# A fused attention and token-mixing kernel: where the dense matmuls of the late odd attention units stand between the logits, weighing and second logits

## The chip, the core and the metric

The kernel runs on one core of a Trainium2 chip. The metric is the device time of one execution in microseconds (us), with all inputs and the output in the chip's main memory. A core has TensorE (matmuls, PE in the profile; its weight loads are PEld), VectorE (DVE), ScalarE (ACT), GpSimd (POOL) and SyncE (SP), which here issues nearly all of the DMAs. Each works through its own list of instructions in order, and they wait for each other by semaphores. TensorE writes into PSUM, which has 8 banks here numbered 0 to 7.

## The reference

One sequence of 2048 tokens with 1024 features. It is normalised (xn), and the output is the sum of the input, an attention branch and a token-mixing branch.

```python
xn = _layernorm(x)                            # x: [1, 2048, 1024] bf16
return x + A(xn, wq, wk, wv, wo, beta) + B(xn, w1, b1, w2, b2)

# A: 32 heads of 32, 4 segments of 512 tokens, one after the other
for s in range(4):
    qs, ks, vs = q[:, :, s], k[:, :, s], v[:, :, s]
    p = softmax(qs @ ks.T * scale + causal_mask)
    a_dot = p @ vs
    a_mem = (phi(qs) @ M) / (phi(qs) @ z + 1e-6)     # memory of the earlier segments
    outs.append(g * a_mem + (1 - g) * a_dot)         # g = sigmoid(beta), one for each head
    M += phi(ks).T @ vs;  z += phi(ks).sum(tokens)
A = concat(outs) @ wo

# B: an MLP over the token dimension
B = (gelu(layernorm(xn).T @ w1 + b1) @ w2 + b2).T    # 2048 -> 3584 -> 2048
```

`phi(t)` is `t + 1` where t > 0, else `exp(t)`.

## The kernel before

First comes branch B (some 390 us). The attention follows, in `attention` (L1531), as a loop over 32 units. Unit u is one segment (u // 8) and one group of four heads (u % 8). Each unit issues, in program order, four kinds of work for TensorE:

- **Logits** (`logits(u, step)`, L1349). Keys times queries of four heads, transposed (keys on partitions), each head on 32 rows of the array, in blocks of 128 keys. Step 0 is key block 0 against 512 queries; step 1 is blocks 1 and 3 (384 and 128 queries); step 2 is block 2 of unit u and of unit u+1 together (256 queries each), so that only even units have a step 2. Each step writes PSUM banks 0 to 3, then one ScalarE instruction (L1370) exponentiates all four banks into pT. GpSimd then zeroes the part above the diagonal of each block (`affine_select`, L1374, the mask). Every logits step waits until the exp of the step before has read the banks. pT has two copies, for even and for odd units.
- **Weighing** of the unit before (`weigh(u - 1, part)`, L1379): many narrow matmuls of pT with the values (and one with the memory for each 128 queries). Part 0 writes bank 4, part 1 bank 5, part 2 bank 4 again, which must have been drained by VectorE (L1424, tile `ost`). Part 1 is the first that needs key block 2 of unit u-1. In the first three segments part 2 also updates the memory (L1435, L1437).
- **Dense jobs**: eight accumulating matmuls 128x512 each, in banks 6 and 7 by turns (`dense(n)`, L1326, issues the next n matmuls of the job queue). They are projections for later units (`q_job`, `k_job`, `v_job`) and output products of finished segments (`wo_job`). At its end each job has its bank read: by ScalarE for qT and vA (L1253, L1299), by VectorE for fin (L1313). The next job but one needs that bank.
- **Side steps**, a queue of VectorE and SyncE work: `combine(u - 1)` (L1440: scales, products, sum), the DMA transpose of its result into oT, the feature map phi of the queries, and others. `dense` takes one of them from the queue when a job reaches one of its stops (L1503, L1504).

How many dense matmuls go where is laid down by `cut(total, shares)` (L1604), which divides the unit's dense matmuls in proportion to a tuple. For an odd unit the places are: ahead of step 0, between step 0 and weighing part 0, between parts 0 and 1, between parts 1 and 2, between part 2 and step 1, and behind step 1. An even unit has one place more, between steps 1 and 2. From unit 18 on a quota (L1502) sets the total: with the jobs at hand an odd unit has 20 dense matmuls, 16 in unit 31. With 20, the third tuple below gives an odd unit 4, 2, 2, 2, 1, 9; with 16, it gives 4, 1, 1, 2, 0, 8. Unit 18 starts at about 531 us, unit 31 at about 627 us. After the loop, `tail` (L1612) weighs the last unit and finishes the last segment's output products; the transposed result of unit 30 is read there by the products that take row block 6 of wo.

```python
            if u >= 18 and even:
                cuts = self.cut(total, (0, 5, 1, 4, 0, 9, 5))
            elif u < 10 or u >= 14 and total <= 26:
                cuts = self.cut(total, (0, 4, 2, 4, 1, 13, 8) if even else (7, 3, 2, 4, 1, 15))
            else:
                cuts = self.cut(total, (0, 4, 2, 2, 2, 14, 8) if even else (7, 3, 2, 2, 2, 16))
```

Of the kernel before, what the change touches and what calls it, by code (L numbers as in the profile page):

```python
# [386 lines left out]
class _Kernel:  # L387
# [1143 lines left out]
    def attention(self):  # L1531
        self.jobs, self.turn, self.left = deque(), 0, 0
        self.side, self.stops = deque(), self.STOPS
        self.exps, self.in_etmp = [], [None] * 4
        self.wo_jobs = deque((c, half) for c in range(4 * (N_SEG - 1)) for half in range(2))
        self.jobs.extend([self.q_job(0), self.k_job(0)] + [self.v_job(0, c) for c in range(4)])
        self.dense(16)
        self.late_exps()
        self.phi_k(0)
        self.k_transpose(0)  # L1540
        self.jobs.extend([self.q_job(1), self.k_job(1)])
        self.dense(100)
        for u in range(N_UNIT):
            if u == N_GRP:
                t, R = _Walk(self.mem, self.B_AT + self.STG_AT, self.B_AT + self.S2_AT).take(
                    "oT2", [P, N_GRP, SEG_L], BF16, N_GRP)
                self.oT.append(t)
                self.R_oT.append(R)
                self.load_fin(0)
                self.load_fin(1)  # L1550
            if 1 <= u <= N_GRP:
                self.fw.dma(self.wo[:, u - 1, :], self.A_wo[(u - 1) * P:u * P, :], writes=[self.R_wo[u - 1]])
            even = u % 2 == 0
            self.jobs.extend(self.unit_jobs(u))
            total = 8 * len(self.jobs) - sum(j[0] for j in self.jobs) - self.left
            xn = self.XN_AT.index(u) + 4 if u in self.XN_AT else None
            if u in self.XN_AT[::4]:
                self.xn_load(xn)
                self.xn_load(xn + 1)
            if u >= 18 and even:  # L1560
                cuts = self.cut(total, (0, 5, 1, 4, 0, 9, 5))
            elif u < 10 or u >= 14 and total <= 26:
                cuts = self.cut(total, (0, 4, 2, 4, 1, 13, 8) if even else (7, 3, 2, 4, 1, 15))
            else:
                cuts = self.cut(total, (0, 4, 2, 2, 2, 14, 8) if even else (7, 3, 2, 2, 2, 16))
            end = u >= N_UNIT - 4
            self.stops = self.STOPS_FEW if total <= 26 and u >= 14 else self.STOPS
            self.dense(cuts[0])
            self.logits(u, 0)
            self.dense(cuts[1], end)  # L1570
            while end and self.side:
                self.side.popleft()()
            if u:
                self.weigh(u - 1, 0)
            self.dense(cuts[2], False)
            if u:
                self.weigh(u - 1, 1)
            self.dense(cuts[3], False)
            if u:
                self.weigh(u - 1, 2)  # L1580
                steps = self.combine(u - 1)
                last = steps[-1]
                steps[-1] = lambda u=u, last=last: (last(), self.o_transpose_dma(u - 1))
                self.side.append(steps.pop(0))
            if N_GRP <= u:
                self.side.append(lambda u=u: self.phi_q(u))
            if u:
                self.side.extend(steps)
            if u + 1 < N_UNIT:
                self.side.append(lambda u=u: (self.phi_k(u + 1), self.k_transpose(u + 1)))  # L1590
            if xn is not None:
                self.side.append(lambda c=xn: (self.xn_scale(c), self.xn_transpose(c), c % 4 < 2 and self.xn_load(c + 2)))
            self.dense(cuts[4])
            self.logits(u, 1)
            if even:
                self.dense(cuts[5])
                self.logits(u, 2)
            self.dense(8 * len(self.jobs) - sum(j[0] for j in self.jobs) - self.left)
        while self.side:
            self.side.popleft()()  # L1600
        self.tail()
# [84 lines left out]
```

## Time and profile before

| | us |
|---|---|
| median of 4 executions (651.43 to 651.85) | 651.59 |
| the profiled execution | 651.64 |
| its span, first to last instruction | 649.9 |
| TensorE busy | 645.4 |
| VectorE busy | 434.7 |
| ScalarE busy | 282.4 |
| GpSimd busy | 152.3 |

The span is some 1.7 us shorter than the time, which includes what lies around the program. The page divides the span into 40 slices of about 16 us, a digit for the busy tenths of each:

```profile
PE   9999999999999999999999999999999999999998
DVE  6885676665556664744637326766887888787896
ACT  6643222232210000110101037778777878889770
POOL 2410000000001220220202203343334444454440
PEclk9999999999999999999999999999999999999999
```

The last 15 or so slices are the attention: VectorE and ScalarE are busy for seven to nine tenths there, less in the stage ahead of it. The groups of instructions with the largest parts in the attention outside TensorE are these (columns: busy us, mean ns of one, then the idle time of the engine ahead of it and what ended most of it):

```profile
L1370 ACT ACTIVATE pT<-ps_all 128x2048 bf16<-128x2048 f32 x80 | 150.2, 1877 | 43.3 <-PE ps_all L199 42.7
L1374 POOL TENSOR_SCALAR_AFFINE_SELECT pT<-pT 128x512 bf16<-128x512 bf16 x128 | 103.8, 829 | 161.6 <-ACT pT L1370 161.6
L1424 DVE TENSOR_TENSOR ost<-ps_all,eps 128x396 bf16<-128x396 f32 (+1 forms) x72 | 36.9, 521 | 26.2 <-PE ps_all L199 25.7
L1473 DVE TENSOR_TENSOR prod<-ost,srec 128x1024 bf16<-128x1024 bf16 (+1 forms) x31 | 35.9, 1159 | 0.3
```

In a timeline the first two columns are the start and the length in us; an `x` with a number is how many instructions of one kind stand in the piece, and a bracket gives the engine's idle time ahead of it and what ended it.

### The profile page before, as it was taken

How to read it: one execution, taken by the hardware profiler on the slowest of the kernel's cores; microseconds unless marked ns; L12 is line 12 of the kernel's file. 1: busy time of each engine (PE TensorE's matmuls, PEld its weight loads, DVE VectorE, ACT ScalarE, POOL GpSimd, SP SyncE). 2: the span in 40 equal slices, each digit the busy share in tenths (PEclk: the TensorE clock that was granted, in tenths of full speed). 3: DMA queues.
4: the chain of work that ended last, by engine and by line, in shares of the span. 5: the costliest groups of instructions: out<-in, count | busy, mean ns of one | idle time of the engine just before them, and what ended most of it. 6: DMA issues, size and time to landing. Idle time of an engine off the chain costs nothing.

```text
span 649.9 us, 11189 instructions
## 1 busy us (share of the span) xinstructions
PE 645.4 (99%) x4611; PEld 303.9 (47%) x4611; DVE 434.7 (67%) x813; ACT 282.4 (43%) x307; POOL 152.3 (23%) x179
## 2 busy tenths in 40 slices
PE   9999999999999999999999999999999999999998
PEld 3444444444444444444444444444455454445544
DVE  6885676665556664744637326766887888787896
ACT  6643222232210000110101037778777878889770
POOL 2410000000001220220202203343334444454440
PEclk9999999999999999999999999999999999999999
DMA  8804233233488947538272957989863675445334
GB/s 302 217 0 131 66 103 92 65 111 85 126 259 196 239 119 210 147 112 227 73 219 84 267 124 179 191 166 215 145 142 94 161 164 123 125 103 129 101 97 139
DMA packets 190123, 95.00 MB, mean 146 GB/s; under 512 B 108664, under 2 KB 176248, under 8 KB 190072
## 3 DMA queue, kind: packets, MB, share of 16 engines
q1 hardware_dynamic: 189928, 94.25, 57.7%
q8 instruction: 36, 0.59, 0.4%
q14 instruction: 15, 0.12, 0.1%
q10 hardware_dynamic: 144, 0.03, 0.0%
HBM read 69.23 MB, written 11.53 MB: 124 GB/s over the span
## 4 chain that ended last, share of the span: by engine, by line
PE 94%; DMA 2%; ACT 2%; DVE 1%; SPq 0%; issue 0%
PE ps_all L199 94%; ACT pT L1370 1%; DMA w2s<-in_B_w_dram 1%; DMA w1early<-in_B_w_dram 1%; DVE sum L648 0%; SPq L221 0%; DVE part L689 0%; ACT qT L1253 0%; ACT vA L1299 0%; DVE gT L663 0%; DVE fin L1632 0%; PE ps_all L205 0%
## 5 line engine op out<-in xcount | busy, mean ns | idle before, releaser
L1370 ACT ACTIVATE pT<-ps_all 128x2048 bf16<-128x2048 f32 x80 | 150.2, 1877 | 43.3 <-PE ps_all L199 42.7
L1374 POOL TENSOR_SCALAR_AFFINE_SELECT pT<-pT 128x512 bf16<-128x512 bf16 x128 | 103.8, 829 | 161.6 <-ACT pT L1370 161.6
L689 DVE TENSOR_TENSOR part<-ps_all,part 128x512 f32<-128x512 f32 x84 | 57.7, 690 | 108.5 <-PE ps_all L199 87.6
L1075 POOL TENSOR_TENSOR part<-part,stg 128x512 f32<-128x512 f32 x24 | 33.0, 1404 | 284.4 <-DVE part L689 284.4
L746 ACT ACTIVATE g<-part,b1c 128x512 f16<-128x512 f32 x36 | 26.0, 722 | 99.0 <-DVE part L689 99.0
L199 PE MATMUL ps_all<-wv,xnT 128*128 128x512 bf16 x256 | 68.5, 380 | 0.4 <-ACT qT L1253 0.2
L199 PE MATMUL ps_all<-xnT,wq 128*128 128x512 bf16 x256 | 66.4, 380 | 0.0
L199 PE MATMUL ps_all<-wo,oT 128*128 128x512 bf16 (+2 forms) x272 | 63.8, 367 | 0.0
L694 ACT ACTIVATE part<-ps_all 128x512 f32<-128x512 f32 x24 | 14.0, 596 | 101.6 <-PE ps_all L199 67.1
L199 PEld LDWEIGHTS ps_all<-vA,pT 128*128 128x128 bf16 x1280 | 45.9, 96 | 19.3 <-DVE ost L1424 1.2
L1424 DVE TENSOR_TENSOR ost<-ps_all,eps 128x396 bf16<-128x396 f32 (+1 forms) x72 | 36.9, 521 | 26.2 <-PE ps_all L199 25.7
L199 PE MATMUL ps_all<-g,sum 128*128 128x512 f16 x224 | 51.0, 379 | 0.0
L199 PE MATMUL ps_all<-g,w2s 128*128 128x512 f16 x224 | 51.0, 379 | 0.0
L199 PE MATMUL ps_all<-gT,sum 128*128 128x512 f16 x224 | 50.3, 379 | 0.1
L199 PE MATMUL ps_all<-vA,pT 128*128 128x33 bf16 x1280 | 48.5, 177 | 0.0
L199 PE MATMUL ps_all<-h,sum 128*128 128x512 f16 x192 | 45.2, 379 | 0.0
L199 PE MATMUL ps_all<-h,w1s 128*128 128x512 f16 x192 | 44.9, 379 | 0.0
L199 PE MATMUL ps_all<-hT,sum 128*128 128x512 f16 x192 | 43.6, 379 | 0.0
L1473 DVE TENSOR_TENSOR prod<-ost,srec 128x1024 bf16<-128x1024 bf16 (+1 forms) x31 | 35.9, 1159 | 0.3
L199 PEld LDWEIGHTS ps_all<-wo,oT 128*128 128x128 bf16 x272 | 23.9, 97 | 24.4 <-issue 3.7
L199 PEld LDWEIGHTS ps_all<-xnT,wq 128*128 128x128 bf16 x256 | 22.5, 97 | 25.4 <-issue 5.3
L199 PEld LDWEIGHTS ps_all<-gT,sum 128*128 128x128 f16 x224 | 21.8, 98 | 26.8 <-DVE gT L663 0.6
(119 smaller groups left out, 863.8 us busy)
## 6 DMA issues: line engine op xcount, KB each, us to landing
w2s<-in_B_w_dram SPq DMA_DIRECT2D x8, 1792.0 KB, 9.7
w1s<-in_B_w_dram SPq DMA_DIRECT2D x12, 1024.0 KB, 5.6
wq<-in_A_wq_dram SPq DMA_DIRECT2D x32, 256.0 KB, 3.3
xs<-in_A_x_dram SPq DMA_DIRECT2D x24, 256.0 KB, 3.4
stg<-in_A_x_dram SPq DMA_DIRECT2D x16, 256.0 KB, 2.9
out_dram<-stg SPq DMA_DIRECT2D x16, 256.0 KB, 4.3
wk<-in_A_wk_dram SPq DMA_DIRECT2D x16, 256.0 KB, 3.4
fin<-out_dram SPq DMA_DIRECT2D x16, 256.0 KB, 3.4
```

The lines of the kernel that those rows point to most:

```text
L199: ins = self.nc.tensor.matmul(*args, **kwargs)
L689: self.fw.op("dve", lambda e: e.tensor_tensor(self.tmp[dst][:], self.bank(b), self.tmp[src][:], op=ALU.add), reads=[self.R_bank[b], self.R ...
L694: self.fw.op("act", lambda e: e.activation(self.tmp[dst][:], self.bank(b), ACT.Copy), reads=[self.R_bank[b]], writes=[self.R_tmp[dst]])
L746: self.fw.op("act", lambda e: e.activation(self.gB[f % 2][half][:, f // 2, :], src, ACT.Gelu_apprx_tanh, bias=self.b1c[:, f:f + 1], scale= ...
L1075: fw.op("pool", lambda e: e.tensor_tensor(self.tmp[t][:], self.tmp[t][:], self.stg[k][:, 512 * half:512 * half + 512], op=ALU.add), reads= ...
L1370: fw.op("act", lambda e: e.activation(dst, src, ACT.Exp, scale=SCALE), reads=self.R_bank[0:4], writes=[R[v % 2][kb] for v, kb, _ in blocks ...
L1374: fw.op("pool", lambda e: e.affine_select(d, d, pattern=[[0, 4], [1, P]], compare_op=ALU.is_ge, fill=0.0, base=0, channel_multiplier=-1), ...
L1424: fw.op("dve", lambda e: e.tensor_tensor(dst, src, eps, op=ALU.add), reads=[self.R_bank[b], self.R_eps], writes=[self.R_ost[o][part]])
L1473: fw.op("dve", lambda e: e.tensor_tensor(self.prod[:, a0:a1], ost[:, a0:a1, 0:D_HEAD], rec[:, a0:a1].unsqueeze(2).to_broadcast([P, a1 - a0 ...
```

## The change

Odd units from 18 on get a tuple of shares of their own. With a total of 20 it gives 4, 1, 2, 1, 0, 12: one dense matmul instead of two between step 0 and weighing part 0, one instead of two between parts 1 and 2, none instead of one between part 2 and step 1, and twelve instead of nine behind step 1. In unit 31, with 16, it gives 3, 1, 2, 0, 0, 10. Seven units are touched: 19, 21, 23, 25, 27, 29 and 31. Because the jobs then end at other places among the side steps, three query-weight loads (in units 19, 23 and 27) are issued by SyncE behind an oT transpose instead of ahead of it, and in unit 31 VectorE's drain of an output job comes behind the drain of weighing part 2 instead of ahead of it. The order on ScalarE and GpSimd is the same.

```diff
--- before.py
+++ after.py
@@ -1559,6 +1559,8 @@
                 self.xn_load(xn + 1)
             if u >= 18 and even:
                 cuts = self.cut(total, (0, 5, 1, 4, 0, 9, 5))
+            elif u >= 18:
+                cuts = self.cut(total, (4, 1, 2, 1, 0, 12))
             elif u < 10 or u >= 14 and total <= 26:
                 cuts = self.cut(total, (0, 4, 2, 4, 1, 13, 8) if even else (7, 3, 2, 4, 1, 15))
             else:
```

## The prediction

> **Names.** In unit u of the attention loop L0, L1 and L2 are the logits steps (L2 in even units only), each a few 32-row matmuls into PSUM banks 0 to 3 and then one exp on ScalarE (L1370). W0, W1, W2 are the three weighing groups of unit u-1, in banks 4, 5 and 4, each drained by VectorE (ost, L1424). "Dense" is one 128x512 matmul of a projection or output job, in banks 6 and 7 by turns.
>
> **What bounds the kernel now.** First the page: TensorE is busy nearly throughout, at full granted clock.
>
> ```profile
> span 649.9 us, 11189 instructions
> PE 645.4 (99%) x4611; PEld 303.9 (47%) x4611; DVE 434.7 (67%) x813; ACT 282.4 (43%) x307; POOL 152.3 (23%) x179
> PE 94%; DMA 2%; ACT 2%; DVE 1%; SPq 0%; issue 0%
> ```
>
> So an edit that neither adds nor removes a matmul can only win back places where TensorE starts late. A matmul's busy time overlaps the next one's, so I looked at starts, not at busy time. Next the chain of waits in order of time, 530 to 610 us (units 18 to 28), where it leaves TensorE:
>
> ```profile
> 552.65 1.88 ACT pT L1370
> 554.53 0.50 ACT qT L1253
> 555.03 0.14 issue
> ...
> 560.68 0.03 issue
> 560.70 0.40 PE ps_all L199 x4
> 561.10 0.09 issue
> ```
>
> ScalarE paces TensorE only at such spots. Third the TensorE timeline, from whose starts I took the length of every piece in units 18 to 31. The end of unit 27 and a piece of unit 28:
>
> ```profile
> 602.13 0.40 PE L199 MATMUL ps_all<-qT,kT 32*128 32x384 bf16 x8
> 602.46 1.25 PE L199 MATMUL ps_all<-xnT,wq 128*128 128x512 bf16 x5
> 603.55 1.03 PE L199 MATMUL ps_all<-wo,oT 128*128 128x512 bf16 x4
> 604.60 0.40 PE L199 MATMUL ps_all<-qT,kT 32*128 32x512 bf16 x4
> ...
> 608.77 0.60 PE L199 MATMUL ps_all<-xnT,wq 128*128 128x512 bf16 x2
> 609.22 1.67 PE L199 MATMUL ps_all<-wo,oT 128*128 128x512 bf16 x7
> 610.83 0.40 PE L199 MATMUL ps_all<-qT,kT 32*128 32x256 bf16 x8
> ```
>
> Nine dense matmuls before logits last 2.14 us in unit 27 (602.46 to 604.60), 2.05 (608.77 to 610.83) in unit 28. Dense matmuls are 0.215 apart, so 9 are 1.94 and the switch to the logits' tiles costs the other 0.11; the further 0.09 is a wait. L1 to exp is 0.45, exp 1.88, and L0 starts 0.14 after its end: 2.47 in all, 0.09 more than TensorE's own 2.38.
>
> All late starts in units 18 to 31, found in this way:
> - (a) 0.09 before L0 of units 20, 22, 24, 26, 28, 30 (behind the odd unit's L1 and nine dense): 0.53 together.
> - (b) after L0 of units 22, 26, 30 (L0 to the next dense 0.49, 0.40, 0.40 for 0.33): 0.16 + 0.07 + 0.07 = 0.30. The dense bank still waits for ScalarE's copy, queued behind the late exp.
> - (c) before W2 of units 20 and 24 (four dense in 0.92 for 0.86): 0.12. VectorE drains W0 late.
> - (d) after L0 of the odd units 21 and 25: 0.25 + 0.16 = 0.41, behind the even unit's L2 exp and a qT copy (the first lines of the chain above).
> Sum 1.36 us, 0.21% of the time: the most that any reordering of these units could win.
>
> [...]
>
> **The change part by part.** Before, an odd unit's 20 dense matmuls fall as 4 L0 2 W0 2 W1 2 W2 1 L1 9; after, as 4 L0 1 W0 2 W1 1 W2 L1 12. Nothing is added or removed; three matmuls (0.645 us) move from between L0 and L1 to behind L1. VectorE (but for one swap in unit 31) and ScalarE keep their order, so no new order is imposed on them.
>
> - *L1 0.645 us earlier; exp earlier.* L1 to L0 of the next unit becomes 0.33 + 12 x 0.215 + 0.11 = 3.02 against the 2.47 the exp needs. (a) goes: -0.53. The copies behind the exp start earlier or as soon as their matmuls end: (b) goes, -0.30. In unit 21, for one:
>
> ```profile
> 558.68 1.88 ACT L1370 ACTIVATE pT<-ps_all 128x2048 bf16<-128x2048 f32 x1 [1.25 <-PE ps_all L199]
> 560.45 0.59 ACT L1299 ACTIVATE vA<-ps_all 128x512 bf16<-128x512 f32 x1
> 560.93 0.60 ACT L1253 ACTIVATE qT<-ps_all 128x512 bf16<-128x512 f32 x1
> ```
>
>   The 1.25 idle holds the 0.645. vA's matmuls end about 1.2 after L1, before the exp does; the copy then ends some 0.6 earlier, ahead of the dense matmul at 561.19. What is late next: nothing until the even unit's own L1.
> - *L1 must still find banks 0 to 3 free.* L0 to L1 becomes 0.33 + 0.215 + 0.36 + 0.43 + 0.42 + 0.215 + 0.79 = 2.76 (unit 21 has its late start (d) on top); exp of L0 needs 2.33 plus at most 0.14. Room 0.29. No cost.
> - *W2 0.43 us earlier against bank 4.* From the end of W0 to W2 there are 0.43 + 0.42 + 0.215 = 1.06 us, before 1.28. VectorE's drain starts 0.19 after W0 and lasts 0.57; TensorE follows 0.06 later (unit 20: drain ends 548.96, W2 549.02): 0.82. Room 0.24. It depends on VectorE being free, which in unit 19 is a near thing:
>
> ```profile
> 540.24 0.68 DVE L1313 TENSOR_TENSOR fin<-ps_all,fin 128x512 bf16<-128x512 f32 x1
> 541.12 0.57 DVE L1424 TENSOR_TENSOR ost<-ps_all,eps 128x396 bf16<-128x396 f32 x1 [0.20 <-PE ps_all L199]
> ```
>
>   The idle 0.20 is eaten by W0's 0.215; the drain then starts at most 0.02 late. Other odd units have 0.3 to 1.4 idle there. No cost.
> - *W1 0.215 earlier against POOL.* It needs the mask of the even unit's L2 block: in unit 19 the third of four masks, done at 540.81; W1 comes at 541.15. Room 0.34. W0's masks were done over a microsecond earlier.
> - *VectorE's combine starts 0.43 earlier* (W2's end). It ends in the even unit's W0 drain, whose lateness is (c); 0.43 less the 0.09 of (a) covers 0.06. (c) goes: -0.12.
> - *SyncE.* In units 19, 23, 27 the query-weight load is now issued behind an oT transpose (that waits for VectorE): 603.74 becomes about 607.7 in unit 27, landing 3.2 later, 610.9; its user, the query job of unit 29, starts about 613.5. kT follows in the same place as before; its user is 4 us or more away. No cost; were it late, TensorE would stand at unit 29 for the difference.
> - *Unit 31 has only 16 dense.* 4 L0 1 W0 1 W1 2 W2 L1 8 becomes 3 L0 1 W0 2 W1 W2 L1 10. There L0 follows L2 of unit 30:
>
> ```profile
> 625.15 0.40 PE L199 MATMUL ps_all<-qT,kT 32*128 32x256 bf16 x8
> 625.48 2.12 PE L199 MATMUL ps_all<-wo,oT 128*128 128x512 bf16 x9
> 627.53 0.39 PE L199 MATMUL ps_all<-qT,kT 32*128 32x512 bf16 x4
> ```
>
>   The exp of L2 ends at 627.47, so L0 can't come earlier with eight dense in front: +0.215. L0 to L1 is then 2.32 for an exp that needs 2.33 + 0.06: +0.06. W2, 0.85 behind W0, against 0.82: nothing. In all +0.28 (bounds 0.2 and 0.5, the latter if each wait ends 0.14 behind its exp). Unit 30's combine now stands behind one more output drain (fin, the swap), whose job ends two dense after L1: about 630.9 plus 0.6, so it runs on 0.65 later than before (630.82). Its oT transpose, issued at 636.3 before and landed 3.1 later at 639.4, then lands about 640.1; the product that reads it starts at 639.85, now 0.28 later at 640.1. Between 0 and 0.3; I take 0, and the 0.3 goes into the range.
>
> Sum: -0.53 - 0.30 - 0.12 + 0.28 = -0.67 us. The profiled execution took 651.64 (span 649.9 and 1.7 around it), the median 651.59; so 650.97, or 650.9 on the median's scale. (d) stays.
>
> **Rivals.**
> - *All late starts go, unit 31 included* (-1.36): 650.2. For: all are late exps or what follows them. Against: (d) hangs on the even unit's L1 and L2, which don't move.
> - *Nothing of (a) to (c) is won, unit 31 costs* (+0.28 to 0.5): 652.0. For: 0.09 could be a fixed cost of L0's two waits (exp and kT's DMA), not lateness. Against: (b) shows real queueing behind the same exp.
> - *Slower: W2 waits for VectorE's drain of W0 in every odd unit.* Decides from a drain that starts 0.43 after W0 (0.19 + the room of 0.24). Unit 20's starts 0.95 after (548.41 against 547.47); that lateness would put 0.5 into each of six units and 0.7 into unit 31, 3.7 in all; less the 0.95 won: about 654.4. For: VectorE and POOL are busiest here, and the masks now move onto other VectorE work. Against: the idle time ahead of the drain.
>
> **How the numbers follow.** Forecast 0.64, all gone 0.08, nothing won 0.16, slower 0.12. 0.2% is 1.3 us, about what a measurement of this kernel can tell from no change; the forecast lies within it. The forecast's own range is 650.5 to 651.4 (a quarter of its parts missing, or the bounds of unit 31 and the tail reached). Range 650.1 to 652.2: the first rival's end and the second's. Faster by over 0.2% takes the first rival and a seventh of the forecast: 0.17. Slower the third and a little of the second: 0.14.
>
> **What would show it.** Right: twelve dense and the switch in about 2.69 before L0 of even units, 0.33 from L0 to dense in units 22, 26, 30, still 0.58 in unit 21. Wrong: gaps before W2 of odd units, L1 waiting for exp outside unit 31, a wait for wq, or a late product in the tail.

## The result and the profile after

| | before | after |
|---|---|---|
| median, us (runs) | 651.48 (52) | 650.76 (34) |
| lowest to highest | 651.33 to 651.87 | 650.61 to 651.22 |
| span of the profiled execution | 649.9 | 649.1 |
| TensorE busy | 645.4 | 644.8 |

The ratio of after to before is 0.9989, with a 95% interval of 0.9984 to 0.9993: 0.7 us faster. That is a tenth of a percent, but the interval does not reach 1. The predicted 650.9 is 0.14 too high; 0.11 of this is the kernel before, whose median was 651.59 when the prediction was made and is 651.48 here. The page of the changed kernel, its span, busy times and the shares of the chain that ended last:

```profile
span 649.1 us, 11186 instructions
PE 644.8 (99%) x4611; PEld 304.3 (47%) x4611; DVE 435.1 (67%) x813; ACT 282.7 (44%) x307; POOL 153.8 (24%) x179
PE 94%; ACT 2%; DVE 2%; DMA 2%; POOL 0%; issue 0%; DVEq 0%
```

The page can't show the cause: the number of matmuls is the same and the shares are nearly so. The chain of waits in order of time, from 530 us to the end of the loop, can (start, length, what the end hung on). Up to 550.04 us it stays on TensorE, then:

```profile
550.07 1.88 ACT pT L1370
...
552.45 1.88 ACT pT L1370
554.32 0.50 ACT qT L1253
554.82 0.14 issue
554.96 24.56 PE ps_all L199 x314
...
584.35 40.20 PE ps_all L199 x479
624.55 0.02 issue
624.57 1.89 ACT pT L1370
626.46 0.05 issue
626.50 13.62 PE ps_all L199 x147
```

Before, the chain also left TensorE ahead of L0 of the even units (at 560.70, for one). After, TensorE runs from 554.96 for 24.56 us and from 584.35 for 40.20 us without a piece of ScalarE. What is left are the exps ahead of units 21 and 25 (the two pieces up to 554.96 and the like at 580) and the one ahead of unit 31. They are the prediction's (d), and what it reckoned as the cost of unit 31.

The TensorE timeline of after, the end of unit 27 (start, length):

```profile
601.04 1.90 PE L199 MATMUL ps_all<-xnT,wq 128*128 128x512 bf16 x8
602.78 1.03 PE L199 MATMUL ps_all<-wo,oT 128*128 128x512 bf16 x4
603.74 0.40 PE L199 MATMUL ps_all<-qT,kT 32*128 32x512 bf16 x4
```

Twelve dense matmuls and the switch took 603.74 - 601.04 = 2.70 us, and did so ahead of all six even units (2.696 to 2.697). Twelve times 0.215 is 2.58, so 0.117 is left for the switch to the logits; nine took 2.14 before, where 9 x 0.215 + 0.117 makes 2.05. The late 0.09 is gone. And the same timeline at the end of unit 30 and the start of unit 31:

```profile
624.45 1.90 PE L199 MATMUL ps_all<-wo,oT 128*128 128x512 bf16 x8
626.50 0.40 PE L199 MATMUL ps_all<-qT,kT 32*128 32x512 bf16 x4 [0.15 <-ACT pT L1370]
```

Eight dense took 2.05 (624.45 to 626.50) where their own time is 8 x 0.215 + 0.117 = 1.84. TensorE stood 0.21 for the exp of L2. This is the one new wait on TensorE that the change made, beside 0.06 at L1 of the same unit, which waits for the exp of L0.

All pieces of units 18 to 31 whose length changed beyond the matmuls moved, by the starts on TensorE:

| place | before | after | difference |
|---|---|---|---|
| (a) dense ahead of L0 of six even units, over their own time | 0.09 each | 0 | -0.53 |
| (b) L0 to the next dense, units 22, 26, 30 | 0.490, 0.401, 0.399 | 0.328, 0.328, 0.327 | -0.31 |
| (c) four dense ahead of W2, units 20 and 24 | 0.922, 0.917 | 0.861, 0.862 | -0.12 |
| (d) L0 to the next dense, units 21 and 25 | 0.577, 0.489 | 0.577, 0.488 | 0 |
| unit 31: L0, and L1 | | late by 0.215 and 0.06 | +0.275 |

The sum is -0.685. The start of the last unit's weighing moved from 634.72 to 633.97, by -0.75, of which 0.03 already stood ahead of unit 18 and about 0.03 are differences of a hundredth here and there.

### The profile page after: what moved, and what is told of

The parts are those of the page before. It is cut to its first block, busy times and chain, and to the rows that moved or that the text cites. A ratio compares the mean times of both kernels' runs of the same rounds, so it can differ in the third digit from the quotient of the medians.

```text
span 649.1 us, 11186 instructions
## 1 busy us (share of the span) xinstructions
PE 644.8 (99%) x4611; PEld 304.3 (47%) x4611; DVE 435.1 (67%) x813; ACT 282.7 (44%) x307; POOL 153.8 (24%) x179
## 4 chain that ended last, share of the span: by engine, by line
PE 94%; ACT 2%; DVE 2%; DMA 2%; POOL 0%; issue 0%; DVEq 0%
PE ps_all L199 93%; ACT pT L1370 2%; DMA w2s<-in_B_w_dram 1%; DVE ln_st L587 1%; DVE sum L648 0%; DMA xin<-in_A_x_dram 0%; DVE h L627 0%; POOL ln_rs L611 0%; DVE part L689 0%; ACT qT L1253 0%; ACT vA L1299 0%; DVE gT L663 0%; DVE ln_mv L590 0%; DVE ln_mv L609 0%; DVE fin L1634 0%
## 5 line engine op out<-in xcount | busy, mean ns | idle before, releaser
L1374 POOL TENSOR_SCALAR_AFFINE_SELECT pT<-pT 128x512 bf16<-128x512 bf16 x128 | 105.2, 840 | 159.3 <-ACT pT L1370 159.3
```

The source lines that it names most:

```text
L1374: fw.op("pool", lambda e: e.affine_select(d, d, pattern=[[0, 4], [1, P]], compare_op=ALU.is_ge, fill=0.0, base=0, channel_multiplier=-1), ...
```

## The experiments

All of them compute the whole reference. The kernel before was timed beside each group of them, with a median of 651.45 for the first four and 651.51 for the last two, so gains are best compared each against its own. Edits are shown against the changed kernel. `u + 1 < N_UNIT` leaves unit 31 as it was before. The traces of these kernels lack 52 of the 4611 matmul records; where one is missing, a piece was measured from the start ahead of it to the start behind it.

**One matmul moved instead of three.** The theory is that room behind L1 is what wins, and that VectorE's combine stays as late as it was, because the matmuls ahead of W2 stay where they were. One rival stands in the text below; the other is the prediction's own, that the 0.09 ahead of L0 is a fixed cost of its two waits.

```diff
-            elif u >= 18:
-                cuts = self.cut(total, (4, 1, 2, 1, 0, 12))
+            elif u >= 18 and u + 1 < N_UNIT:
+                cuts = self.cut(total, (4, 2, 2, 2, 0, 10))
```

> Odd units 19 to 29 get 4, 2, 2, 2, 0, 10 (only the dense matmul between weighing part 2 and step 1 goes behind step 1; weighing stays where it was), unit 31 as before the change. Theory (the odd unit's second exp must be over before the next unit's first logits and bank copies): ten dense make 0.33 + 10 x 0.215 + 0.11 = 2.59 us between the two logits starts against 2.47 that the exp needs, so the late starts before L0 of the even units go (-0.53) and those after L0 of units 22, 26, 30 nearly go (-0.27); VectorE's chain is no earlier, so the late W2 of units 20 and 24 grows by 0.09 each: in sum about -0.62, near 650.9. Rival (the gain comes from the weighing and VectorE's combine being earlier): no gain, 651.5.

Measured: 650.83 (650.67 to 651.25), before 651.45; ratio 0.9991, interval 0.9984 to 0.9997. One moved matmul (0.215) covers the whole lateness of 0.09, and (a) is gone. Of (b), 0.04 stays in unit 22 (0.369 from L0 to dense). The waits of L0 are the same two as before, so the 0.09 was lateness and no fixed cost. But the combine isn't earlier now, while the even units come 0.09 sooner. The timeline of TensorE in unit 20:

```profile
547.83 0.81 PE L199 MATMUL ps_all<-wv,xnT 128*128 128x512 bf16 x3
548.85 0.57 PE L199 MATMUL ps_all<-vA,pT 128*128 128x33 bf16 x16 [0.21 <-DVE ost L1424]
```

and that of VectorE in the same kernel and place:

```profile
547.64 0.68 DVE L1313 TENSOR_TENSOR fin<-ps_all,fin 128x512 bf16<-128x512 f32 x1
548.24 1.03 DVE L1424 TENSOR_TENSOR ost<-ps_all,eps 128x396 bf16<-128x396 f32 x2
```

W2 (the 16 narrow ones at 548.85) came 1.02 after the dense matmuls ahead of it began, where it takes 0.86 when nothing is late; TensorE stood for the drain (ost) that VectorE began only at 548.24, behind fin. (One of the four dense records is missing.) So (c) grew from 0.06 to 0.157 in each of units 20 and 24, that is by the 0.09 that had been won ahead of them. -0.53 for (a), -0.27 for (b) and +0.19 for (c) make -0.61; -0.62 was measured.

**Only the matmuls between the weighing groups moved**, to between W2 and L1. This moves W2 as the change does, but not L1.

```diff
-            elif u >= 18:
-                cuts = self.cut(total, (4, 1, 2, 1, 0, 12))
+            elif u >= 18 and u + 1 < N_UNIT:
+                cuts = self.cut(total, (4, 1, 2, 1, 3, 9))
```

> Odd units 19 to 29 get 4, 1, 2, 1, 3, 9: the weighing is as early as in the changed kernel, but step 1 stays where it was before, with nine dense behind it; unit 31 as before the change. Theory: only the late W2 of units 20 and 24 goes, -0.12: 651.35; 0.09 before L0 of the even units and the late starts after it stay. Rival (weighing and combine earlier are the gain): as the changed kernel or better, 650.5 to 650.8.

Measured: 651.34 (651.13 to 651.72), before 651.45; ratio 0.9998, interval 0.9990 to 1.0006, so the time alone can't tell it from before. The starts can. The end of unit 27 on TensorE:

```profile
602.12 1.25 PE L199 MATMUL ps_all<-xnT,wq 128*128 128x512 bf16 x5
603.21 1.03 PE L199 MATMUL ps_all<-wo,oT 128*128 128x512 bf16 x4
604.26 0.40 PE L199 MATMUL ps_all<-qT,kT 32*128 32x512 bf16 x4
```

Nine dense again take 2.14 (602.12 to 604.26). (a) stays in all six units, and so does (b), with 0.490, 0.400 and 0.398; the lateness of W2 in units 20 and 24 is gone. So the earlier W2 of the odd units wins (c) by itself and nothing else; (a) and (b) need the earlier L1, as the experiment above had it.

**The change with unit 31 as it was.**

```diff
-            elif u >= 18:
+            elif u >= 18 and u + 1 < N_UNIT:
                 cuts = self.cut(total, (4, 1, 2, 1, 0, 12))
```

> The changed kernel with unit 31 as before the change (4, 1, 1, 2, 0, 8). Theory: unit 31's new cuts cost 0.28 us (0.215 because its first logits wait for the exp of unit 30, 0.06 at its second logits), so this one is at 650.45 to 650.5. Rival (unit 31 costs nothing, or its combine behind the output drain delays the tail more): 650.75, or below 650.3.

Measured: 650.45 (650.28 to 650.76), before 651.45; ratio 0.9985, interval 0.9978 to 0.9991. This kernel wins 1.00 on its own before, the changed one 0.72, so unit 31 costs 0.28 (0.31 if the two medians are set against each other directly). The starts show 0.275.

**No dense matmul from W0 to L1.** This takes away the cover that the drain of bank 4 has, to see whether the rival's mechanism (W2 waiting for VectorE in odd units) exists and where it sets in.

```diff
-            elif u >= 18:
-                cuts = self.cut(total, (4, 1, 2, 1, 0, 12))
+            elif u >= 18 and u + 1 < N_UNIT:
+                cuts = self.cut(total, (4, 2, 0, 0, 0, 14))
```

> Odd units 19 to 29 get 4, 2, 0, 0, 0, 14: no dense matmul between the three weighing parts; unit 31 as before the change. Theory: W2 needs bank 4 drained, 0.82 us behind the end of W0, and now comes 0.42 behind it, so TensorE waits 0.40 in each of six units: 2.4 above the kernel with unit 31 as before, about 652.9. Rival (the drain is not what W2 waits for, or VectorE catches up): below 651. Rival (VectorE is late in this stage by as much as in unit 20, 0.76): 1.1 in each unit, about 657.

Measured: 654.19 (653.99 to 654.28, four executions), before 651.45; ratio 1.0042, interval 1.0028 to 1.0055. Slower as expected, but by 1.3 us more than was reckoned. TensorE in unit 19:

```profile
541.75 0.57 PE L199 MATMUL ps_all<-vA,pT 128*128 128x33 bf16 x16 [0.24 <-DVE ost L1424]
...
543.32 1.89 PE L199 MATMUL ps_all<-xnT,wq 128*128 128x512 bf16 x8
545.42 0.82 PE L199 MATMUL ps_all<-wo,oT 128*128 128x512 bf16 x3 [0.21 <-ACT vA L1299]
```

and ScalarE of the same kernel behind it:

```profile
543.00 1.88 ACT L1370 ACTIVATE pT<-ps_all 128x2048 bf16<-128x2048 f32 x1 [0.87 <-PE ps_all L199]
544.77 0.59 ACT L1299 ACTIVATE vA<-ps_all 128x512 bf16<-128x512 f32 x1
```

The first wait, ahead of the 16 narrow ones of W2, is the expected one: the three weighing groups take 1.98 from W0 to L1 in unit 19 instead of 1.57, and are 0.41 late in each of the six units, 2.46 in all. The second wait wasn't expected. With 4 + 2 matmuls ahead of W0 and none from there to L1, the eight of the value job end behind L1 in units 19, 23 and 27. Its copy (vA) then stands behind the exp, at 544.77, where the changed kernel has it ahead of the exp, at 541.99; and the next job but one (wo, at 545.42) needs that bank: 0.386 three times, 1.16. Together 3.62, less the 0.95 that (a) to (c) win: 651.45 + 2.67 = 654.12. The change's own 4 + 1 + 2 + 1 are just the eight of that job, so the vA copy is through ahead of the exp.

**One of the eight behind W2 instead of between W0 and W1.** It takes 0.215 of the room of W2, and should use up the 0.24 almost wholly.

```diff
-            elif u >= 18:
-                cuts = self.cut(total, (4, 1, 2, 1, 0, 12))
+            elif u >= 18 and u + 1 < N_UNIT:
+                cuts = self.cut(total, (4, 1, 1, 1, 1, 12))
```

> As the kernel with unit 31 as before, but odd units 19 to 29 get 4, 1, 1, 1, 1, 12: W2 then stands 0.85 us behind the end of W0 (1.06 in the changed kernel), step 1 where it is. Theory: the drain of bank 4 takes 0.82, so there is just no wait: 650.45, up to 0.1 more. Rival (VectorE or the mask is late here, so that the room was nearer to nothing than 0.24): 0.1 to 0.2 in each of six units, 651.0 to 651.6.

Measured: 650.52 (650.29 to 651.04), before 651.51; ratio 0.9985, interval 0.9979 to 0.9992, a gain of 0.99 where the kernel without this edit had 1.00. In unit 19, W0 ended at 540.40 and W2 began at 541.25, 0.85 later with no wait; VectorE's drain took 0.57 from 540.59, so that with TensorE's 0.06 behind it W2 could have come at 541.22. That is 0.03 of room; the second matmul that the change has there makes it the 0.24 of the prediction. The other five units have no wait there either.

**The value job first.** Left over is (d): the exp of L2 in units 20 and 24 starts late because ScalarE copies vA between the exps of L1 and L2. If the even unit finishes the value job's matmuls ahead of L1, and the two units' other shares make up for it, that copy comes ahead of L1's exp.

```diff
-            if u >= 18 and even:
+            if u in (20, 24):
+                cuts = self.cut(total, (0, 5, 1, 6, 0, 9, 3))
+            elif u in (21, 25):
+                cuts = self.cut(total, (6, 1, 2, 1, 0, 10))
+            elif u >= 18 and even:
                 cuts = self.cut(total, (0, 5, 1, 4, 0, 9, 5))
-            elif u >= 18:
+            elif u >= 18 and u + 1 < N_UNIT:
                 cuts = self.cut(total, (4, 1, 2, 1, 0, 12))
```

> As the kernel with unit 31 as before, but in units 20 and 24 two dense matmuls move from behind step 2 to ahead of weighing part 2 (0, 5, 1, 6, 0, 9, 3), so that the value job ends before step 1 and the query job before step 2, and units 21 and 25 get 6, 1, 2, 1, 0, 10. Theory: the 0.25 and 0.16 us after the first logits of units 21 and 25 are a qT copy queued behind an exp, itself behind an exp and a vA copy; with vA copied in ScalarE's idle time ahead of step 1's exp, both go: 0.41 off, 650.05. Rival (it is ScalarE's work in the unit that is too much, not its order): the wait turns up at another logits step, 650.3 to 650.6.

Measured: 650.13 (649.97 to 650.35), before 651.51; ratio 0.9979, interval 0.9971 to 0.9987. This is the fastest of all, ahead of the kernel before and the changed one. ScalarE around units 20 and 21, first in the kernel with only unit 31 undone:

```profile
549.79 1.88 ACT L1370 ACTIVATE pT<-ps_all 128x2048 bf16<-128x2048 f32 x1 [1.67 <-PE ps_all L199]
551.56 0.59 ACT L1299 ACTIVATE vA<-ps_all 128x512 bf16<-128x512 f32 x1
552.17 1.88 ACT L1370 ACTIVATE pT<-ps_all 128x2048 bf16<-128x2048 f32 x1
553.94 0.59 ACT L1253 ACTIVATE qT<-ps_all 128x512 bf16<-128x512 f32 x1
```

then in this one:

```profile
549.41 0.60 ACT L1299 ACTIVATE vA<-ps_all 128x512 bf16<-128x512 f32 x1 [1.07 <-PE ps_all L199]
550.45 1.88 ACT L1370 ACTIVATE pT<-ps_all 128x2048 bf16<-128x2048 f32 x1 [0.44 <-PE ps_all L199]
552.27 0.60 ACT L1253 ACTIVATE qT<-ps_all 128x512 bf16<-128x512 f32 x1
552.83 1.88 ACT L1370 ACTIVATE pT<-ps_all 128x2048 bf16<-128x2048 f32 x1
```

Above, L1's exp, vA, L2's exp and qT follow each other without idle time, and the dense matmul behind L0 waits for the last of them. Below, vA sits in idle time ahead of the exp. L0 to the next dense is 0.327 in units 21 and 25 instead of 0.577 and 0.488. A new 0.04 stands behind L0 of unit 22, since only ten dense cover the exp there. 0.41 less 0.04 is 0.37. Measured, this kernel wins 1.38 on its own before and the one with only unit 31 undone 1.00, a difference of 0.38. So it was the order of ScalarE's work, and not its amount.

## Why the prediction was right

- **The sum.** -0.67 was predicted; the starts give -0.685 and the medians -0.72. The prediction took 1.3 us as about the least that can be told from no change; here the interval is 0.3 us to each side. Each large term holds by itself: (a) -0.53 for -0.53, (b) -0.31 for -0.30, (c) -0.12 for -0.12, and (d) stays to the hundredth. For unit 31, 0.28 was predicted, and the kernel that leaves it alone gives 0.28. The two exps it was put down to are seen in the trace, 0.215 and 0.06.
- **Why (a) goes.** Twelve dense took 2.697, close to the 2.69 laid down. The step held in every stretch without a wait (0.215 to 0.217 from start to start in units 18 to 31, and 0.225 to 0.227 for the first one behind logits), and that made it possible to find waits of 0.06 us from starts alone. The rival that the 0.09 was fixed fell with the first experiment, where ten dense had none of it.
- **Why (b) goes.** ScalarE in unit 21 of the changed kernel:

```profile
557.83 1.88 ACT L1370 ACTIVATE pT<-ps_all 128x2048 bf16<-128x2048 f32 x1 [0.61 <-PE ps_all L199]
559.61 0.59 ACT L1299 ACTIVATE vA<-ps_all 128x512 bf16<-128x512 f32 x1
```

  The copy vA now ends at 560.20, ahead of the dense matmul behind unit 22's L0 (560.74). Before, it ended at 561.04, and that matmul came at 561.19. The 0.84 are the 0.645 moved and the 0.2 already won ahead of the unit.
- **Why (c) goes.** TensorE in unit 20, before:

```profile
548.10 1.02 PE L199 MATMUL ps_all<-wv,xnT 128*128 128x512 bf16 x4
549.02 0.57 PE L199 MATMUL ps_all<-vA,pT 128*128 128x33 bf16 x16
```

  and after:

```profile
547.97 1.02 PE L199 MATMUL ps_all<-wv,xnT 128*128 128x512 bf16 x4
548.83 0.56 PE L199 MATMUL ps_all<-vA,pT 128*128 128x33 bf16 x16
```

  W2 comes 0.86 behind the start of the four dense instead of 0.92. VectorE's drain of W0 began 0.46 earlier, at 547.95 instead of 548.41, and W2 itself only 0.19 earlier.
- **The room of W2.** It was predicted as 0.24. In the changed kernel's unit 19, VectorE's timeline reads:

```profile
540.21 0.68 DVE L1313 TENSOR_TENSOR fin<-ps_all,fin 128x512 bf16<-128x512 f32 x1
540.87 0.57 DVE L1424 TENSOR_TENSOR ost<-ps_all,eps 128x396 bf16<-128x396 f32 x1
```

  The idle time ahead of the drain is just used up, as reckoned. The drain ended at 541.44, and W2 began at 541.74 behind its dense matmul; less TensorE's 0.06 that is 0.24. The slower rival needed a drain later by more than this, and two experiments bracket the point: with 0.215 of the room gone (one of the eight behind W2) there is no wait, and with 0.645 gone (no dense matmul from W0 to L1) there are 0.41 in each unit. The rival's mechanism is real, but the change does not reach it.
- **The rooms of L1 and W1.** No L1 outside unit 31 waits for an exp, and no W1 for a mask: W0 to L1 is the sum of its matmuls in all six units (2.21 in units 19, 21 and 23, 1.98 in 25, 27 and 29, that is by two dense matmuls, 0.43, less than the 2.64 and 2.41 before).
- **SyncE.** In unit 27 the query-weight load was issued at 606.47, where 607.7 was reckoned, behind the transpose (issued at 605.23, 1.20 long). It is 2.7 later than before (603.74), and no matmul waits for it. The 607.7 was the end of the transpose before the change (issued at 606.50, just as long); the prediction had left out that the transpose itself comes earlier.
- **The tail: the 0 was luck.** The prediction left 0 to 0.3 open for the transposed result of unit 30, and took 0. VectorE began that unit's combine 0.36 earlier than before (at 630.46), but was through with it 0.07 later, at 634.97, while TensorE needed the result 0.75 earlier, at about 639.1. Yet the transpose was issued at 635.52, 0.8 earlier than before, and landed at 638.49, so no product waits. What gave the time back is the instruction ahead of the transpose in SyncE's queue. After:

```profile
635.04 0.43 SPq L221 DMA_DIRECT2D fin<-out_dram  x1
635.52 1.20 SPq L221 DMA_TRANSPOSE oT<-o_s  x1
```

  and before:

```profile
634.98 1.31 SPq L221 DMA_DIRECT2D fin<-out_dram  x1
```

  The prediction had taken the issue of this load as it was in one trace. Had it lasted 1.31 again, the transpose would have landed some 0.9 later, at about 639.4: an estimate from these times, and a wait of about 0.3 for TensorE, which would have left some 0.4 of the gain. Why the issue was short wasn't tried.

What the prediction did not see is that the tuple's 4 + 1 + 2 + 1 hold the value job whole ahead of L1. It cost nothing here, but there was nothing to spare: a fourth matmul moved would have put the end of that job behind L1 in units 19, 23 and 27. With six ahead of L1 instead of eight, that cost 1.16 us; with seven it wasn't tried.

## What to carry to other kernels

When one engine is busy throughout, list its late starts one by one against the natural step of its instructions, and ask of each whether the edit moves the thing that it waits for; here four groups of 0.06 to 0.25 us, found in this way, gave the sum to a few hundredths. Moving work from ahead of a step to behind it is free until what was hidden under it (a drain, a copy) has less room than its own time (here nothing was lost with 0.03 of room left, and 0.41 in each unit with 0.645 taken from a room of 0.24), so write down that room for each buffer beforehand. And watch where a job ends relative to a long instruction on the engine that copies its result: a copy of 0.59 us put behind an exp of 1.88 cost 0.386 each time, and put ahead of it won 0.16 to 0.25.

## What was not expected of the hardware

- A DMA issue on SyncE isn't of one length: the same load of fin took 0.43 us of the queue in one kernel and 1.31 in the other, issued within 0.06 us of the same time. From 530 to 636 us each of the two traces has nine such loads issued one by one: before, seven took 0.43, the others 1.39 (at 623.29) and this 1.31; after, eight took 0.43 and one 1.11 (at 622.09). The cause stays open.
- Each start of logits behind dense matmuls cost TensorE 0.117 beyond their steps (twelve steps of 0.215 and the start of the logits made 2.697), with no wait that the trace shows, in every unit where nothing was late. Dense matmuls ahead of a weighing group show no such extra: there the tile is 128*128 on both sides, and four of them took 0.861 and 0.862 ahead of W2 in units 20 and 24. The traces do not show what makes the 0.117, and it wasn't tried.
